# Attention by whole tiles beside the first product, with another order of decoding and another end

## The chip, the cores and the metric

One core of a Trainium2 chip runs the kernel. The metric is the device time of one execution in microseconds. TensorE multiplies matrices, VectorE and GpSimd compute element by element, ScalarE evaluates functions and copies, SyncE issues most transfers. Each engine works through its own instructions in order and waits on semaphores for the others.

## What is computed

Attention within chunks of 64 tokens, for 8 batches of 8 heads with 576 tokens of 64 values, and then two products with a function between them, twice:

```python
scores = scale * np.matmul(q_c, k_c.transpose(0, 1, 2, 4, 3))   # in chunks of 64
scores = scores - np.max(scores, axis=-1, keepdims=True)
attn = np.exp(scores)
attn = attn / (np.sum(attn, axis=-1, keepdims=True) + 1e-09)
out = np.matmul(attn, v_c)
# x: 4608 tokens x 512
h = x @ w_in; r = np.maximum(h, 0.0); x = (r * r) @ w_out       # 512 -> 2048 -> 512
h = x @ w_in2                                                    # 512 -> 2048
g = np.where(h >= 1, h, np.where(h <= -1, 0.0, (h + 1) ** 2 / 4))
return g @ w_out2                                                # 2048 -> 512
```

The weights arrive as float64 and are decoded from their bits in the kernel.

## The kernel before, in words

The tokens of the attention stand in 36 tiles of 128 tokens; a tile has two units of four heads each (`UT` = 2, 72 units). A unit goes through steps: A (`att_a`, line 285) transposes q and k with four 128x128 transposes into one PSUM bank; `att_ae` copies them out on ScalarE; B (`att_b`) makes the scores with sixteen 64x64 products and takes their maximum on VectorE; `att_exp` (line 322) makes four exponentials on ScalarE with their sums; `att_n` inverts the sums on VectorE and scales on GpSimd; C (`att_c`) transposes twice, `att_ce` copies out; D (`att_d`) weighs v with sixteen 64x64 products; `att_x` (line 374) splits the result on ScalarE and VectorE into a rounded part xh and a rest xl, the input of the first product.

The first product (`plain_h`, line 400) runs in 9 blocks of 512 tokens. For each of 16 pieces of weights (`fi`) it makes two slots of six products of 128x128 by 128x512, called ph in the profile; after the second slot ScalarE takes the relu into a buffer g, GpSimd squares it, and SyncE stores it. Two PSUM banks take turns (`h0`, `h1`); the g buffers are a ring of six (`RG`, line 397). The pieces of the first product's weights are decoded in three steps: `piece_a` (an absolute value on ScalarE and three bit operations on VectorE, lines 111 to 118), `piece_b` (a product on VectorE, line 147, and a cast on ScalarE, line 150), `piece_c` (a subtraction on GpSimd). One call of `decode` (line 671) takes step c of one piece, b of the next and a of the one after, and loads the piece two ahead into one of two staging buffers `ws`. The weights of the three later products are decoded in 48 units (m, a, b) in the same way (`unit_a` to `unit_d`, lines 174 to 219): four parts, three sums of them on GpSimd, a rounded part and a rest of seven columns, stored to DRAM and loaded by `load_w` (line 243) as tiles for TensorE when a product is near.

The order is written out by hand. A head of eleven turns does the attention of the first four tiles and the first decoding calls. Then a list of slots follows: slot 2 (16 j + fi) + c is one half of a product step of block j. In each slot come the six products, then a decoding call if one is due (`PACE`), then what `at_slot` has put there. A turn of one unit takes four slots: D, B and x in the first, the exponentials in the second, C with its copy and the normalization in the third, A with its copies and the loads of q, k and v in the fourth. Decoding units start at slot 22 (`U0`) and come every 5.1 slots.

```python
            if n_dec[0] < NF + 2 and n_dec[0] < len(DEC) + 1 + PACE * ((s + 2) // 2):
                decode()
```

The second product (`form_b`, w = 0), the third (`form_a`) and the fourth (`form_b`, w = 1) run after slot 288 (`SB1`) in five pairs of token halves with seven products each instead of eight (P1 to P7). At the end of the last, the result goes through `store` (line 600): VectorE transposes it in blocks of 32, and SyncE stores it in four transfers.

Of the kernel before, what the change touches and what calls it, by code (L numbers as in the profile page):

```python
# [15 lines left out]
P = 128  # L16

TINY = 2.0**-15 * 1.125
CH = 64
# [7 lines left out]
CIDX = {"P1": 0, "P2": 1, "P7": 2, "P4": 3, "P5": 4, "P6": 5, "P3": 6}  # L27
# [4 lines left out]
def chunk_attention_moe_moe2(ctx, tc, q, k, v, w_in1, w_out1, w_in2, w_out2, out):  # L32
# [72 lines left out]
    win = {}  # L105
    wst = {}
# [17 lines left out]
    def wy():  # L124
        n_y[0] += 1
        return rt(4 + n_y[0] % 3, [P, 4 * P], "wy", U32)
# [54 lines left out]
    def sums(c):  # L181

        for o, x, z, op in ((4, 2, 3, ALU.add), (2, 0, 2, ALU.subtract), (5, 4, 0, ALU.subtract), (6, 1, 5, ALU.subtract)):
            nc.gpsimd.tensor_tensor(out=c[:, o], in0=c[:, x], in1=c[:, z], op=op)
# [21 lines left out]
    def unit_c(*u):  # L206
        c = wst[u]
        hi = ep.tile([P, 7, P], F32R, tag="wh", name="wh", bufs=2)
        nc.scalar.copy(hi, c)
        wst[u] = (c, hi)  # L210

    def unit_hi(m, a, b):
        nc.sync.dma_start(out=wd[m, a][:, 0, b], in_=f(wst[m, a, b][1]))

    def unit_d(m, a, b):
        c, hi = wst.pop((m, a, b))
        lo = ep.tile([P, 7, P], F32R, tag="wl", name="wl", bufs=2)
        nc.vector.tensor_tensor(out=lo, in0=c, in1=f(hi), op=ALU.subtract)
        nc.sync.dma_start(out=wd[m, a][:, 1, b], in_=f(lo))
# [21 lines left out]
    wt = {}  # L241

# [7 lines left out]
    att = {}  # L250
# [45 lines left out]
    def att_ae(u):  # L296
        qkT = ep.tile([P, 2, NP, P], F32, tag="qkT", name="qkT", bufs=2)
        nc.scalar.activation(out=qkT[:, 0], in_=att[u][:, 0], func=AF.Copy, scale=SCALE)
        nc.scalar.copy(qkT[:, 1], att[u][:, 1])
        att[u] = qkT  # L300

    def att_b(u):

        qkT = att[u]
        pt = pa.tile([P, 2, 512], F32, tag="qk", name="psB")
        for p in range(NP):
# [9 lines left out]
        sc = pt[:, :, 0:2 * CH].rearrange("q e (c k) -> q e c k", c=2)  # L316
        m = ep.tile([P, 2, 2], F32, tag="m", name="m", bufs=3)
        z = ep.tile([P, 2, 2], F32, tag="z", name="z", bufs=3)
        nc.vector.tensor_reduce(out=m, in_=sc, op=ALU.max, axis=AX.X, negate=True)
        att[u] = [sc, m, z]  # L320

    def att_exp(u):
        sc, m, z = att[u]
        s = ep.tile([P, 2, 2, CH], F32, tag="s", name="s", bufs=2)
        for e in range(2):
            for c in range(2):
# [6 lines left out]
                )  # L333
        att[u] = [s, z]

    def att_n(u):
        s, z = att[u]
        nc.vector.tensor_scalar_add(z, z, 1e-9)
        nc.vector.reciprocal(z, z)
        s4 = s.rearrange("q e c k -> q (e c) k")  # L340
        z4 = z.rearrange("q e c -> q (e c)")
        nc.gpsimd.tensor_tensor(out=s4, in0=s4, in1=z4.unsqueeze(2).to_broadcast([P, HU, CH]), op=ALU.mult)

    def att_c(u):
        s, _ = att[u]
        pt = pa.tile([P, 2, NP, CH], F32, tag="t", name="psC", padded_shape=[P, HU, 2, CH], bufs=2)
        for e in range(2):
            nc.tensor.transpose(  # L348
                pt[:, e].rearrange("k p t -> k (p t)"), s[:, e].rearrange("q c k -> q (c k)"), ident
            )  # L350
        att[u] = pt

    def att_ce(u):
        at = ep.tile([P, 2, NP, CH], F32, tag="atT", name="atT", bufs=2)
        nc.scalar.copy(at, att[u])
        att[u] = at

    def att_d(u):

        at = att[u]  # L360
        pt = pa.tile([P, 2, 512], F32, tag="d", name="psD")
        for p in range(NP):
            for c in range(2):
                for e in range(2):
                    nc.tensor.matmul(  # L365
                        pt[rows(e), c, p * CH:(p + 1) * CH],
# [5 lines left out]
        att[u] = pt  # L372

    def att_x(u):
        pt = att.pop(u)
        (xh, xl), a, n = unit_x(u)[0]
        o = pt[:, :, 0:NP * CH].rearrange("d c (p t) -> d p c t", p=NP)
        xh, xl = (x.rearrange("d p (c t) -> d p c t", c=2) for x in (xh, xl))
        nc.scalar.copy(xh, o)
        nc.vector.tensor_tensor(out=xl, in0=o, in1=f(xh), op=ALU.subtract)  # L380
# [16 lines left out]
    RG = tuple(range(7, 13))  # L397
# [167 lines left out]
    def form_b(w, j, prod, kk):  # L565
# [20 lines left out]
        for dp in range(2):  # L586
            c = c_tile(n)
            if key is None:
# [11 lines left out]
    def store(j, dh, th, dp, c):  # L600
# [5 lines left out]
        for a in range(P // G):  # L606
            nc.sync.dma_start(
# [10 lines left out]
    LB, LC, LD, LV = 1, 2, 3, 0  # L618
    PER = 4
    DEC = (1, 2, 4, 6, 8, 10)  # L620
    PACE = 0.78
    U0, UPER = 22, 5.1
# [28 lines left out]
    with tc.manual_schedule():  # L651
# [14 lines left out]
        strokes = []  # L666
        for p in range(NF):
            strokes.append([(piece_a, p), (piece_b, p), (piece_c, p)])
        n_dec = [0]

        def decode():
            n = n_dec[0]
            n_dec[0] += 1
            if 0 <= n - 2 < NF:
                piece_c(n - 2)
            if 0 <= n - 1 < NF:
                piece_b(n - 1)
# [5 lines left out]
        def turn(i):  # L683

            res = [[] for _ in range(4)]

            def put(n, fn, u):
                if 0 <= u < NU:
                    res[n].append((fn, (u,)))

            put(0, att_d, i - LD)
            put(0, att_b, i - LB)
            put(0, att_x, i - LD)
            put(1, att_exp, i - LB)
            put(2, att_c, i - LC)
            put(2, att_ce, i - LC)
            put(2, att_n, i - LB)
            put(3, att_a, i)
            put(3, att_ae, i)
            if i >= LV and (i - LV) % UT == 0 and i - LV < NU:  # L700
                res[3].append((load_v, ((i - LV) // UT,)))
            if i % UT == UT - 1 and i // UT + QB < NU // UT:
# [197 lines left out]
```

## Time and profile before

| | |
|---|---|
| time, median of 3 runs | 1622.3 us (1620.76 to 1623.78) |
| time of the profiled execution | 1622.09 us |
| its span, first to last instruction | 1620.3 us |
| TensorE busy | 1586.6 us (98%) |
| VectorE, ScalarE, GpSimd busy | 1089.7, 868.5, 413.3 us |

Times in the rows below count from the start of the span. PE is TensorE, PEld its weight loads, DVE VectorE, ACT ScalarE, POOL GpSimd, SP SyncE. A busy TensorE is not one at its peak, since products are pipelined: starts matter more than durations. L451 is a line of the kernel.

### The profile page before, as it was taken

The numbers are of one execution on the slowest core, as the hardware profiler recorded it, in microseconds if no ns is written. First come the engines' busy times: TensorE is split into PE (matmuls) and PEld (weight loads), VectorE is DVE, ScalarE is ACT, GpSimd is POOL, SyncE is SP. The second block draws the span as 40 slices with busy tenths as digits, with TensorE's granted clock in tenths as the row PEclk, the third lists the DMA queues.
The fourth block names the chain that finished last, engine by engine and source line by source line (L and its number), as shares of the span: only waits on it lengthen the run. The fifth ranks groups of instructions, "written<-read, shape, count | busy, mean of one in ns | idle before, by whom it ended". The sixth has DMA issues, their size and how long they took to land.

```text
span 1620.3 us, 27342 instructions
## 1 busy us (share of the span) xinstructions
PE 1586.6 (98%) x9504; PEld 1362.6 (84%) x9504; DVE 1089.7 (67%) x1437; ACT 868.5 (54%) x1852; POOL 413.3 (26%) x461
## 2 busy tenths in 40 slices
PE   7889999999999999999999999999999999999998
PEld 5667777777778899999888898898888899998887
DVE  5956666665443376777677666857574787877786
ACT  7656666666553344344444566666665434444442
POOL 2657666665444200000000333333220000000000
PEclk9999999999999999999999999999999999999999
DMA  9769999999996982625378665574679773563723
GB/s 213 204 185 295 291 290 287 293 302 281 277 301 205 318 250 91 216 62 190 110 219 254 210 230 178 190 238 159 240 244 337 248 199 99 129 170 83 207 37 49
DMA packets 442730, 339.47 MB, mean 210 GB/s; under 512 B 214240, under 2 KB 419040, under 8 KB 442592
## 3 DMA queue, kind: packets, MB, share of 16 engines
q1 hardware_dynamic: 442592, 337.73, 69.3%
q8 instruction: 75, 1.23, 0.3%
q14 instruction: 63, 0.52, 0.1%
HBM read 195.04 MB, written 142.61 MB: 208 GB/s over the span
## 4 chain that ended last, share of the span: by engine, by line
PE 87%; DVE 5%; ACT 2%; DMA 2%; issue 2%; POOL 1%; SPq 0%; DVEq 0%; ACTq 0%; POOLq 0%
PE X L451 34%; PE ph L409 23%; PE V L451 17%; PE W L451 8%; PE psA L291 1%; PE psD L365 1%; PE psB L309 1%; DVE ol L441 1%; DVE t L532 1%; PE psC L348 1%; DMA ws<-in_moe_w_in_dram 1%; ACT s L327 1%; DVE wy L115 1%; DVE xr L445 0%; DVE wy L118 0%
## 5 line engine op out<-in xcount | busy, mean ns | idle before, releaser
L451 PE MATMUL X<-oh,w 128*128 128x448 f32 (+1 forms) x1920 | 557.5, 371 | 1.5 <-DVE c L512 1.5
L440 ACT CAST oh<-gr 128x896 fp32r<-128x896 f32 (+1 forms) x280 | 270.0, 964 | 334.1 <-PE X L451 160.5
L441 DVE TENSOR_TENSOR ol<-gr,oh 128x896 fp32r<-128x896 f32 (+1 forms) x280 | 314.5, 1124 | 182.6 <-ACT oh L440 175.3
L451 PEld LDWEIGHTS X<-oh,w 128*128 128x128 f32 x1920 | 360.0, 188 | 43.8 <-DVE c L512 1.9
L451 PE MATMUL X<-ol,w 128*128 128x448 f32 (+1 forms) x960 | 356.4, 371 | 4.2 <-DVE ol L441 4.2
L451 PE MATMUL V<-oh,w 128*128 128x448 f32 (+1 forms) x960 | 278.5, 371 | 0.0
L409 PE MATMUL ph<-xh,ih 128*128 128x512 f32 x576 | 245.3, 426 | 0.0
L409 PE MATMUL ph<-xl,ih 128*128 128x512 f32 x576 | 227.9, 396 | 0.0
L409 PE MATMUL ph<-xh,il 128*128 128x512 f32 x576 | 227.8, 395 | 0.0
L422 POOL TENSOR_TENSOR g<-g 128x512 f32<-128x512 f32 x144 | 171.3, 1189 | 143.6 <-ACT g L421 140.5
L451 PEld LDWEIGHTS X<-ol,w 128*128 128x128 f32 x960 | 180.1, 188 | 26.7 <-DVE ol L441 6.3
L451 PEld LDWEIGHTS V<-oh,w 128*128 128x128 f32 x960 | 180.2, 188 | 20.9
L445 DVE TENSOR_TENSOR gr<-gr,gr 128x896 f32<-128x896 f32 (+1 forms) x160 | 177.9, 1112 | 3.7 <-DMA gr<-g 3.7
L451 PE MATMUL V<-ol,w 128*128 128x448 f32 (+1 forms) x480 | 178.0, 371 | 0.0
L421 ACT ACTIVATE g<-ph 128x512 f32<-128x512 f32 x144 | 86.4, 600 | 134.8 <-PE ph L409 123.3
L451 PE MATMUL W<-oh,w 128*128 128x448 f32 (+1 forms) x480 | 139.4, 371 | 0.0
L409 PEld LDWEIGHTS ph<-xl,ih 128*128 128x128 f32 x576 | 109.3, 190 | 24.7
L409 PEld LDWEIGHTS ph<-xh,ih 128*128 128x128 f32 x576 | 109.4, 190 | 21.6
L409 PEld LDWEIGHTS ph<-xh,il 128*128 128x128 f32 x576 | 110.0, 191 | 16.6
L526 ACT ACTIVATE t<-c,half 128x448 f32<-128x448 f32 (+1 forms) x120 | 81.3, 681 | 70.9 <-DVE c L512 70.8
L441 POOL TENSOR_TENSOR ol<-xr,oh 128x896 fp32r<-128x896 f32 (+1 forms) x10 | 23.7, 2374 | 360.7 <-ACT oh L440 353.0
L532 DVE SCALAR_TENSOR_TENSOR t<-c,t 128x448 f32<-128x448 f32 (+1 forms) x120 | 96.4, 830 | 18.4 <-ACT t L526 18.2
(69 smaller groups left out, 1906.0 us busy)
## 6 DMA issues: line engine op xcount, KB each, us to landing
w<-w SPq DMA_DIRECT2D x168, 256.0 KB, 5.1
gr<-g SPq DMA_DIRECT2D x96, 448.0 KB, 5.2
gr<-g SPq DMA_DIRECT2D x64, 480.0 KB, 4.6
g<-t SPq DMA_DIRECT2D x96, 224.0 KB, 2.7
wu<-in_moe_w_out_dram SPq DMA_DIRECT2D x64, 256.0 KB, 4.6
g<-t SPq DMA_DIRECT2D x64, 240.0 KB, 4.4
w<-wh SPq DMA_DIRECT2D x32, 448.0 KB, 4.1
w<-wl SPq DMA_DIRECT2D x32, 448.0 KB, 5.0
```

The lines of the kernel that those rows point to most:

```text
L115: nc.vector.scalar_tensor_tensor(out=y, in0=w1, scalar=0xC0000000, in1=y, op0=ALU.bitwise_and, op1=ALU.bitwise_or)
L291: nc.tensor.transpose(pt[:, i, p, :], qkn[i][:, h0 + 2 * p:h0 + 2 * p + 2, :].rearrange("p h d -> p (h d)"), ident)
L309: nc.tensor.matmul(pt[rows(p), e, c * CH:(c + 1) * CH], qkT[rows(e), 0, p, rows(c)], qkT[rows(e), 1, p, rows(c)], start=True, stop=True,)
L409: nc.tensor.matmul(ph, win[fi][wi][:, kt * P:(kt + 1) * P], x[:, i, :], start=(kt == 0 and a == 0), stop=(kt == KT - 1 and a == 2),)
L421: nc.scalar.activation(out=g, in_=ph, func=AF.Relu)
L422: nc.gpsimd.tensor_tensor(out=g, in0=g, in1=g, op=ALU.mult)
L440: nc.scalar.copy(hi, raw)
L441: eng.tensor_tensor(out=lo, in0=raw, in1=f(hi), op=ALU.subtract)
L445: eng.tensor_tensor(out=o, in0=x, in1=z, op=ALU.subtract)
L451: nc.tensor.matmul(o, wt_[:, wi, c, :], x[:, i, :], start=first and a == 0, stop=last and a == 2, skip_group_check=True,)
L526: nc.scalar.activation(out=t, in_=h, func=AF.Square, bias=half, scale=0.5)
L532: nc.vector.scalar_tensor_tensor(out=t, in0=h, scalar=1.0, in1=t, op0=ALU.max, op1=ALU.min)
```

## The change

In the loop beside the first product attention goes by tiles of two units: eight transposes in A into two banks, 32 products in B and in D, four transposes in C, one maximum over both units, the exponentials in two groups of four, one normalization. A tile takes eight slots (`PER` = 8). D of a tile and B of the next stand in one slot, x and the first four exponentials in the same slot, the other four in the next, the normalization four slots after B, C six after, A four before the next B. The head does the first four tiles by units as before, and A, B and the exponentials of the fifth by a whole tile.

Decoding gets a step more: the cast on ScalarE (`piece_h`) and GpSimd's subtraction come one call later each. In a slot it now stands behind the attention. Seven calls fall in the head instead of six, `PACE` is 0.8 instead of 0.78, units start at slot 28 and come every 5 slots. A fourth buffer y comes from the ring of g, which keeps five. For the second product's weights (m = 0) the three products P1, P5 and P6 are written straight into TensorE's tiles by `unit_c` and `unit_d`; only the other four columns go to DRAM, and 24 of 168 loads fall away. In the last store of the kernel VectorE transposes from PSUM without a copy, and every second transfer is issued by ScalarE.

```diff
-CIDX = {"P1": 0, "P2": 1, "P7": 2, "P4": 3, "P5": 4, "P6": 5, "P3": 6}
+CIDX = {"P1": 0, "P2": 1, "P7": 2, "P4": 3, "P3": 4, "P5": 5, "P6": 6}
...
-        return rt(4 + n_y[0] % 3, [P, 4 * P], "wy", U32)
+        return rt(4 + n_y[0] % 4, [P, 4 * P], "wy", U32)
...
+    def piece_h(p):
+        y, hi, lo = wst[p]
         nc.scalar.copy(hi, f(y))
...
+    def unit_c(m, a, b):
+        c = wst[m, a, b]
+        if m == 0:
+            for prod in RANK[:3]:
+                if b == 0:
+                    wt[0, a, prod] = wp.tile([P, 2, 2, P], F32R, tag=f"w{w_tag(RANK.index(prod) * HF + a)}", name="w0")
+                nc.scalar.copy(wt[0, a, prod][:, 0, b], c[:, CIDX[prod]])
+        r = unit_r(m)
+        hi = ep.tile([P, r.stop - r.start, P], F32R, tag="wh", name="wh", bufs=2, padded_shape=[P, 7, P])
+        nc.scalar.copy(hi, c[:, r])
+        wst[m, a, b] = (c, hi)
+    def unit_r(m):
+        return slice(1, 5) if m == 0 else slice(0, 7)
...
+        if m == 0:
+            for prod in RANK[:3]:
+                t = wt[0, a, prod]
+                nc.vector.tensor_tensor(out=t[:, 1, b], in0=c[:, CIDX[prod]], in1=f(t[:, 0, b]), op=ALU.subtract)
+        lo = ep.tile([P, r.stop - r.start, P], F32R, tag="wl", name="wl", bufs=2, padded_shape=[P, 7, P])
+        nc.vector.tensor_tensor(out=lo, in0=c[:, r], in1=f(hi), op=ALU.subtract)
+        nc.sync.dma_start(out=wd[m, a][:, 1, b, r], in_=f(lo))
...
+    def tile_a(t):
+        att[t, "a"] = []
+        for i in range(2):
+            pt = pa.tile([P, UT, NP, P], F32, tag="t", name="psA", bufs=2)
+            for h in range(0, H, 2):
+                nc.tensor.transpose(
+                    pt[:, h // HU, h // 2 % NP, :], qks[t][i][:, h:h + 2, :].rearrange("p h d -> p (h d)"), ident
+                )
+            att[t, "a"].append(pt)
...
+    def tile_b(t):
+        pt = pa.tile([P, 2, 512], F32, tag="qk", name="psB")
+        for i in range(UT):
+            scores(pt[:, :, i * 2 * CH:(i + 1) * 2 * CH], qkT_of(t * UT)[:, i])
+        att[t, "b"] = maxima(pt, UT * 2)
+    def tile_exp(t, e):
+        exps(s_of(t * UT), *att[t, "b"], (e,), UT * 2)
...
-    RG = tuple(range(7, 13))
+    RG = tuple(range(8, 13))
...
+            if key is None and w == 1 and j == NPAIR - 1:
+                store(j, dh, th, dp, o[dp])
+                continue
...
-            nc.sync.dma_start(
+            (nc.scalar if j == NPAIR - 1 and th == 0 and a % 2 else nc.sync).dma_start(
...
-    PER = 4
-    DEC = (1, 2, 4, 6, 8, 10)
-    PACE = 0.78
-    U0, UPER = 22, 5.1
+    PER, PH = 8, 4
+    DEC = (1, 2, 3, 5, 7, 9, 10)
+    PACE = 0.8
+    U0, UPER = 28, 5
...
+            for d, fn in ((3, piece_c), (2, piece_h), (1, piece_b)):
+                if 0 <= n - d < NF:
+                    fn(n - d)
...
+        for t in range(T0_, NTI):
+            g = PER * (t - T0_ - 1) + PH
+            if t > T0_:
+                at_slot(g - 4, tile_a, t)
+                at_slot(g - 4, tile_ae, t)
+                at_slot(g - 4, load_v, t)
+                if t + QB < NTI:
+                    at_slot(g - 4, load_qk, t + QB)
+                at_slot(g, tile_b, t)
+                at_slot(g, tile_x, t - 1)
+                at_slot(g, tile_exp, t, 0)
+                at_slot(g + 1, tile_exp, t, 1)
+                at_slot(g + 4, tile_n, t)
+            at_slot(g + 6, tile_c, t)
+            at_slot(g + 6, tile_ce, t)
+            at_slot(g + PER, tile_d, t)
+        at_slot(g + PER, tile_x, t)
...
-            s = 2 * NF * (NBL - 3) + 2 * t if t < 24 else 2 * NF * (NBL - 1) + 2 * (t - 24) + 1 if t < 32 else SB1 + t - 30
-            at_slot(s, load_w, 0, tag, kk, RANK[r])
+            if t >= 24:
+                s = 2 * NF * (NBL - 1) + 2 * (t - 24) + 1 if t < 32 else SB1 + t - 30
+                at_slot(s, load_w, 0, tag, kk, RANK[r])
...
-            if n_dec[0] < NF + 2 and n_dec[0] < len(DEC) + 1 + PACE * ((s + 2) // 2):
-                decode()
             i = 0
...
+            if n_dec[0] < NF + 3 and n_dec[0] < len(DEC) + 1 + PACE * ((s + 2) // 2):
+                decode()
```

## Rows read from the trace of the kernel before

**Rows 1.** Windows: stretch, TensorE and other engines' busy us, granted clock, DMA share, GB/s.
```profile
39.00:130.00 91.00, 79.88 (x661) 62.13 (x658) 68.60 (x106) 53.75 (x175) 56.95 (x55) 0.92 0.69 198
130.00:500.00 370.00, 370.00 (x3232) 293.37 (x3223) 222.17 (x406) 232.26 (x797) 218.53 (x274) 1.00 0.95 289
551.50:1613.10 1061.60, 1055.92 (x5040) 944.51 (x5039) 764.11 (x858) 538.20 (x729) 106.61 (x96) 1.00 0.60 181
```

**Rows 2.** TensorE's timeline (start, us, what, idle before), chain (start, us), a window.
```profile
52.71 0.70 PE L365 MATMUL psD<-atT,vt 64*64 64x64 f32 x16 [3.67 <-ACT atT L355]
...
98.97 0.73 PE L309 MATMUL psB<-qkT 64*64 64x64 f32 x16 [5.01 <-ACT qkT L299]
...
54.47 5.06 PE ph L409 x12
...
99.70 4.67 PE ph L409 x12
...
54.40:59.00 4.60, 4.60 (x15) 3.63 (x12) 4.53 (x6) 2.36 (x10) 3.74 (x3) 0.50 0.53 163
```

**Rows 3.** VectorE's groups, 39 to 100 (busy us, mean ns), and ScalarE's timeline.
```profile
L118 DVE SCALAR_TENSOR_TENSOR wy<-ws,wy 128x512 uint32<-128x512 uint32 x11 | 12.0, 1087 | 0.4
L115 DVE SCALAR_TENSOR_TENSOR wy<-ws,wy 128x512 uint32<-128x512 uint32 x11 | 11.7, 1065 | 0.4
L112 DVE TENSOR_SCALAR wy<-ws 128x512 uint32<-128x512 uint32 x11 | 10.5, 957 | 1.0 <-DMA ws<-in_moe_w_in_dram 1.0
L147 DVE SCALAR_TENSOR_TENSOR wy<-ih,wy 128x512 f32<-128x512 f32 x11 | 8.7, 794 | 0.1
...
97.22 0.67 ACT L111 ACTIVATE wa<-wu 128x512 f32<-128x512 f32 x1 [4.49 <-DMA wu<-in_moe_w_out_dram]
```

**Rows 4.** Chain of waits near the loop's end (start us, us, what).
```profile
487.10 1.39 PE ph L409 x6
488.49 0.44 PE psA L291 x4
488.93 1.40 PE ph L409 x6
490.32 0.39 PE psD L365 x16
490.71 0.29 PE psB L309 x14
491.00 2.95 PE ph L409 x12
493.95 0.22 PE psC L348 x2
494.17 2.77 PE ph L409 x12
496.94 0.39 PE psD L365 x16
```

**Rows 5.** Head: chain (start, us) and TensorE's timeline.
```profile
13.86 1.29 ACT s L327 x8
...
29.42 0.73 PE L309 MATMUL psB<-qkT 64*64 64x64 f32 x16
...
39.01 0.79 PE L409 MATMUL ph<-xh,ih 128*128 128x512 f32 x1
```

**Rows 6.** End: chain (start, us) and SyncE's queue.
```profile
1613.12 0.57 ACT c L589
...
1613.77 4.09 SPq L607 DMA_DIRECT2D out_dram<-ct  x8
```

**Rows 7.** Groups from 130 to 500 (busy us, mean ns, idle before).
```profile
L421 ACT ACTIVATE g<-ph 128x512 f32<-128x512 f32 x105 | 63.0, 600 | 89.3 <-PE ph L409 84.5 <-DMA g<-g 3.0 <-DMA qkn<-in_k_dram 1.5
...
L342 POOL TENSOR_TENSOR s<-s,z 128x256 f32<-128x256 f32 x52 | 42.8, 823 | 32.0 <-DVE z L339 13.3 <-PE ph L409 6.1 <-PE psA L291 3.8
...
L319 DVE TENSOR_REDUCE m<-psB 128x4 f32<-128x256 f32 x52 | 22.0, 422 | 76.2 <-PE psB L309 76.0
```

More of the change, by code (lines that the diff above doesn't have):

```diff
@@ L105, in chunk_attention_moe_moe2, with w_tag @@
     win = {}
+    wt = {}
+    def w_tag(t):
+        return (t + 2 * NF) % 56
     wst = {}
@@ L246, in load_w, with of_tile, qkT_of, s_of @@
         wt[m, a, prod] = t
-    att = {}
+    att, ttile = {}, {}
+    def of_tile(name, u, shape, bufs=1):
+        if (name, u // UT) not in ttile:
+            ttile[name, u // UT] = ep.tile(shape, F32, tag=name, name=name, bufs=bufs)
+        return ttile[name, u // UT]
+    def qkT_of(u):
+        return of_tile("qkT", u, [P, UT, 2, NP, P])
+    def s_of(u):
+        return of_tile("s", u, [P, 2, UT * 2, CH], SBUFS)
+    def at_of(u):
+        return of_tile("atT", u, [P, UT, 2, NP, CH])
     def rows(par):
@@ L315, in att_b, with maxima, exps @@
                     )
[L316 to L318 removed]
+    def maxima(pt, n):
+        sc = pt[:, :, 0:n * CH].rearrange("q e (c k) -> q e c k", c=n)
+        m = ep.tile([P, 2, n], F32, tag="m", name="m", bufs=3, padded_shape=[P, 2, UT * 2])
+        z = ep.tile([P, 2, n], F32, tag="z", name="z", bufs=3, padded_shape=[P, 2, UT * 2])
         nc.vector.tensor_reduce(out=m, in_=sc, op=ALU.max, axis=AX.X, negate=True)
[L320 to L326, printed above, removed]
+        return [sc, m, z]
+    def exps(s, sc, m, z, es, n):
+        for e in es:
+            for c in range(n):
                 nc.scalar.activation(
@@ L351, in att_c, with tile_c, tile_ce @@
         att[u] = pt
     def att_ce(u):
-        at = ep.tile([P, 2, NP, CH], F32, tag="atT", name="atT", bufs=2)
-        nc.scalar.copy(at, att[u])
-        att[u] = at
+        nc.scalar.copy(at_of(u)[:, u % UT], att[u])
+    def tile_c(t):
+        att[t, "c"] = pt = pa.tile([P, UT, 2, NP, CH], F32, tag="t", name="psC", bufs=2)
+        for i in range(UT):
+            turned(pt[:, i], s_of(t * UT), i)
+    def tile_ce(t):
+        nc.scalar.copy(at_of(t * UT), att.pop((t, "c")))
     def att_d(u):
-        at = att[u]
@@ L681, in decode @@
                     stage_piece(n + 2)
[L683 to L702, printed above, removed]
-                res[3].append((load_qk, (i // UT + QB,)))
-            return res
         def tiles_until(j):
@@ L720, in head @@
             do(att_d, i - LD)
+            if i == n0:
+                tile_a(T0_)
             do(att_exp, i - LB)
             do(att_ae, i)
+            if i == n0:
+                tile_ae(T0_)
             do(att_ce, i - LC)
+            if i == n0 + 1:
+                for e in range(2):
+                    tile_exp(T0_, e)
             if i in DEC:
```

120 lines of the change are left out of this document (66 added, 54 removed).

## The prediction

> **What bounds the kernel now.** I read busy time by stretch first, then the waits of TensorE, then the chain of waits where TensorE stands still. From 551.5 to 1613.1 TensorE is busy 1055.9 of 1061.6 us [rows 1]: the second and third products leave under 6 us, and the change hardly touches their order. From 130 to 500 it is busy 370.0 of 370.0 us [rows 1]. So there only fewer or shorter TensorE instructions help. From 39 to 130 it is busy 79.9 of 91.0 us [rows 1]: 11.1 us of waits in the first block. In that block the reader is to see two long waits, 3.67 us for a copy of atT and 5.01 us for qkT, both late on ScalarE [rows 2]. Behind each the granted clock falls to 0.50, the 1.2 GHz level: twelve products then take 5.06 and 4.67 us [rows 2], against 2.95 at full clock [rows 4]. That is 2.1 + 1.7 = 3.8 us more, so the first block loses 14.9 us in all. ScalarE is late because its in-order queue holds a decoding step that waits for VectorE, and VectorE spends 0.957 + 1.065 + 1.087 + 0.794 = 3.9 us on each of eleven pieces between 39 and 100 [rows 3]. For the second wait it holds the first step of a unit, which stood 4.49 us for its load [rows 3].
>
> **Whole tiles.** One unit's turn on TensorE is read from one stretch of the chain. D takes 0.39 us, B behind it 0.29, and the twelve products after them 2.95 where twelve after a C take 2.77: 0.18 more [rows 4]. Where D runs alone it is 0.39 again, so the sixteen small products of B are worth 0.29, and D, which has sixteen of the same size, about 0.29 + 0.10. Entering and leaving the 64x64 form therefore costs 0.10 + 0.18 = 0.28 us a time. C (two transposes) takes 0.22. A (four) takes 0.44 and the products around it 1.39 + 1.40 instead of 2.77 [rows 4], about 0.46: both are near 0.11 a transpose, with next to nothing per group. So a tile of two units saves one 0.28 and nothing on transposes: 31 tiles x 0.28 = 8.7 us. One D that stood alone goes too (0.28). Against it, the loop gets one more A and one more C, since the head did eleven A and nine C and will do ten and eight: 0.46 + 0.22 = 0.7. Net **-8.3 us**. Ends: nothing saved, +0.7, if a block of 64 small products costs as much as two of 32; and -13, if the transposes share 0.07 a group as well. I take the middle value, since B's 0.29 was read with and without a neighbour.
>
> **New waits in that loop.** At full clock a slot of six products is 2.77 / 2 = 1.39 us. The exponentials of half a tile now stand on ScalarE ahead of the relu of the pair of slots that ends next, where one unit's four stood behind it; behind them wait that relu, its square on GpSimd, and the PSUM bank that TensorE wants again three slots (4.2 us) after B. The maximum over twice the width takes up to 2 x 0.42 us [rows 7], four exponentials 1.29 [rows 5], a relu 0.60 [rows 7]: 2.7 us. So VectorE may come 1.4 us late before TensorE stands. It sat idle before 52 maxima for 76.2 us in all, 1.5 each [rows 7], so it is mostly early. The other wait: the normalization is issued at the tile's slot + 4 and C at + 6, 2.8 us apart. GpSimd needs 2 x 0.82 = 1.6 us for it [rows 7], and a square or the four sums of a unit may stand ahead. With sums right before it C waits about 1 us; the period of five slots against eight puts them there in one unit of eight, four times. I take **+1.0 us** for this stretch, ends 0 and +31 (1 us at each tile).
>
> **First block.** Units now start at slot 28 instead of 22, behind the last decoding, and their first loads two to three slots ahead of that. So the 4.49 us wait for the load on ScalarE goes, with the late GpSimd and SyncE work around it. Attention stands ahead of decoding in a slot, and ScalarE's cast of a piece comes one call later than VectorE's product for it, so ScalarE no longer stands for a product just issued. What is late next is VectorE itself. Seven decoding calls fall in the head and one each in slots 0, 1, 2, 4, 6. From 41 us on VectorE has four first parts (3 x about 1.04 = 3.1 us each) and three second parts (0.8) ahead of the maximum of slot 4 [rows 3], 14.8 us, and 1.2 of attention: it comes at 57. TensorE ends that B at 41 + 1.3 (half clock at the start) + 5 x 1.39 + A 0.92 + C 0.44 + 1.44 = 52. Late by 5 us, less the 1.4 of slack: a wait of about 3.5 us. At slot 12 VectorE has 13.9 us more and TensorE 3.5 + 8 x 1.39 + 2.8 = 17.4: on time. A wait of 3.67 us brought the lower clock [rows 2], so I add half of its 2.1 us: 4.5 us are left of 14.9, **-10.4 us**. Ends: all goes, -14.9, and none, 0. The ring of g buffers falls from six to five, 17 instead of 21 us for relu, square and store; in the first block a store came late in SyncE's queue, which counts for the upper end. Decoding loads of ws stay two ahead and stand in the same queue as the g stores, as now.
>
> **Head.** In the head a decoding call more (eight to ten: seven calls for six) and a tile's A and B replace three units' A and two units' B. From the B at 29.42 to the first product at 39.01 it is 9.6 us now [rows 5]. After the change: B 0.73, maximum 0.42, exponentials 1.29 and about 0.4 of decoding; the copies of eight transposes (four take 0.44 at full clock [rows 4], twice that here) end about 4.2 us after that B; then a B of twice 0.73, a maximum of 0.84, eight exponentials 2.6, two decoding steps on ScalarE 1.2, xh and xl 0.8, D 0.7: 11.8 with overlaps taken off about 11.5. **+1.9 us**, ends 0 and +4.
>
> **In-place weights.** For 24 tiles of the first three products the loads (256 KB each) fall away, and the stores of 16 units shrink from seven columns to four. ScalarE gets three copies of a 128x128 for each unit and a cast over four instead of seven, VectorE three subtractions. No load of a weight ends a TensorE wait between 130 and 551, and ScalarE and VectorE are busy 232 and 222 of 370 us there [rows 1], so the added work, at most 0.7 us for 16 units, is covered: 0. Uncovered it would be +10; if a transfer gets clear of it, -1.
>
> **End.** The last two copies to SBUF go (0.57 on the path [rows 6]), as VectorE transposes from PSUM, and every second of the eight last stores is issued by ScalarE. Now SyncE issues eight in 4.09 us, 0.51 each [rows 6], and the span ends 2.4 us after the last issue. Halved, 2.0 us go if issuing sets the pace, none if the transfers do. Between 0.6 and 2.6 I take **-2.0**, nearest to the issue row. The Trainium skill's page DMA: Bandwidth & Descriptors (Issuing engines are not separate DMA queues) says the contrary in weight: all issuers share the same sixteen DMA engines, and a second issuer saves only the sequencer's time, usually small. Here issue was 4.09 us of the last 7.2, so the trace agrees only in the mechanism; by the page's "small" the sum would be 1605.5.
>
> **The sum.** The profiled run took 1622.1 us by the clock of the times (span 1620.3), 0.2 under the median 1622.3. 1622.1 - 8.3 - 10.4 + 1.0 + 1.9 + 0 - 2.0 = 1604.3: forecast **1604**.
>
> **Rivals.**
> 1. VectorE stays the bound of the first block. For: 3.9 us a piece, and five calls nearly in a row at the loop's start. Against: units no longer overlap with decoding. Nothing is gained there: 1604 + 10.4 = 1614.
> 2. The first block runs without a wait and transposes share their group cost: 1604 - 4.5 - 4.5 = 1595. For: attention is ahead of decoding in each slot. Against: the maximum is still queued behind earlier slots' decoding.
> 3. Slower: relu behind exponentials. In each tile VectorE comes late with the maximum, the exponentials hold the relu, and TensorE stands for the bank. The gains without the loop's new waits are 19 us, so it decides from 19 / 31 = 0.6 us a tile. At 1.5 us a tile: 1604 - 1 + 46 = 1649; at 0.8, 1628. Against: no wait of TensorE in 370 us now, and 1.5 us of idle time ahead of a maximum.
> 4. The change doesn't do what it says: a merged B and D still drain at every unit. Then 8.7 + 0.3 us stay: 1613.
>
> **Chances.** Forecast 0.53 (its own range 1598 to 1610), rival 1 0.15, rival 2 0.14, rival 4 0.08, rival 3 0.10. The range 1593 to 1618 takes in all but rival 3 and the edges of the others. A difference of 0.2%, 3.2 us, is about what can be told here. Faster 0.86 (all but rival 3, less 0.04 of stray in rivals 1 and 4), same 0.05, slower 0.09.
>
> **What would show it.** Right: D and B in one block of 64 small products near 1.4 us, and a period of a tile near 13.8 us where two turns take 14.1; TensorE waits under 6 us between the first product and 130, and none of 5 us; first product of weights near 41; last transposes right behind the last product and the span ending about 5 us later. Wrong: waits of the first kind of product for a relu in every tile, waits of C for the normalization, or a granted clock of 0.50 behind a wait after 60 us.

## The result, and the profile after

The changed kernel takes 1635.1 us (median of 4 runs, 1630.9 to 1636.7), the kernel before beside it 1622.0 (1620.8 to 1623.8): 1.0079 of the time before, 95% interval 1.0065 to 1.0092. It is slower by 13 us where the forecast was 18 us faster. The profiled execution has a span of 1633.4 us against 1620.3.

First the windows that answer to [rows 1] (columns as there):

```profile
39.00:130.00 91.00, 77.52 (x668) 61.62 (x669) 64.79 (x91) 53.25 (x177) 50.27 (x45) 0.98 0.67 182
130.00:500.00 370.00, 352.94 (x3117) 285.08 (x3115) 233.64 (x364) 228.25 (x742) 219.26 (x248) 0.99 0.88 251
564.10:1627.10 1063.00, 1056.49 (x5041) 944.59 (x5039) 765.18 (x858) 537.70 (x728) 106.87 (x96) 1.00 0.60 181
```

The reader is to see the middle row: TensorE, busy for all of these 370 us before, now stands 17 us of them. The third row, 1063.0 against 1061.6 us, is nearly as it was. The names in the rows: psA to psD are the PSUM tiles that steps A to D write, qkT and atT ScalarE's copies of A and C; s are the exponentials, z the sums and their inverse; wu is a unit of weights as loaded, wa its absolute value, wc its four parts and three sums. What TensorE waits for stands in its waits (waiting line, what it waits for: us in total, times, longest):

```profile
PE psC L420 <- POOL s L395: 21.8, 19, 2.4
PE ph L506 <- ACT g L518: 5.6, 2, 4.6
...
PE psD L451 <- DVE xl L467: 3.9, 2, 3.4
...
PE psD L451 <- ACT atT L438: 1.9, 1, 1.9
```

The wait of the transposes C for GpSimd's normalization is new in this size: before it was 1.4 us in four.

```profile
PE psC L348 <- POOL s L342: 1.4, 4, 0.4
```

TensorE's timeline gives the rest of the account, by the start of B in three tiles (start us, us, what; the windows end inside B, so durations and counts are not those of its 32 products):

```profile
54.26 0.45 PE L366 MATMUL psB<-qkT 64*64 64x64 f32 x15
...
75.00 0.56 PE L366 MATMUL psB<-qkT 64*64 64x64 f32 x20
...
407.47 0.73 PE L366 MATMUL psB<-qkT 64*64 64x64 f32 x31
```

And the chain of waits where nothing disturbs it, which answers to [rows 4] (start us, us, what):

```profile
455.90 2.74 PE ph L506 x12
458.64 0.44 PE psC L420 x4
459.08 2.77 PE ph L506 x12
461.85 0.62 PE psD L451 x32
462.48 0.57 PE psB L366 x29
463.05 5.69 PE ph L506 x24
468.74 0.87 PE psA L345 x8
469.61 2.74 PE ph L506 x12
```

A tile's period is 469.61 - 455.90 = 13.71 us. D and B are one block of 1.19 us, where two units took 2 x (0.39 + 0.29) = 1.36 [rows 4]. From 75.00 to 407.47 there are 22 tiles; at 13.71 they would take 301.6 us and they take 332.5, so **30.8 us** are lost. The first tile, 54.26 to 75.00, takes 20.74: **7.0 us** lost. Of the 30.8, TensorE stands 22.4 us; the lower clock behind two of the waits takes some 3.6 more, and the rest is not resolved. The account of the 13.1 us, profiled run against profiled run:

| stretch | forecast | measured |
|---|---|---|
| head: first product at 43.60, before 39.01 | +1.9 | +4.6 |
| whole tiles: loop (520.5, before 512.3) less its losses (37.8, before 14.9) | -8.3 | -14.7 |
| first block's losses (7.0, before 14.9) | -10.4 | -7.9 |
| waits and lost clock from 75 to 407 us | +1.0 | +30.8 |
| second to fourth products (1063.0, before 1061.8) | 0 | +1.3 |
| last matmul to the end (6.3, before 7.2) | -2.0 | -0.9 |

The loop ends with the first instruction of the second product, at 564.08 us after and 551.33 before. The rows split at 75 us, where the forecast's first block ran to 130: some 6 of the 30.8 us lie between 75 and 130. On the forecast's own stretch the first block still loses about 13 of its 14.9 us, and the loop behind it about 25. One row is wrong by far. Its mechanism is read in one tile: timelines of VectorE, ScalarE, GpSimd and TensorE from 151 to 165 us (start us, us, what, idle time before and what ended it):

```profile
152.30 0.69 DVE L378 TENSOR_REDUCE m<-psB 128x8 f32<-128x512 f32 x1 [2.49 <-PE psB L366]
152.91 0.41 DVE L467 TENSOR_TENSOR xl<-psD,xh 128x256 fp32r<-128x256 f32 x1
...
158.30 0.69 DVE L205 SCALAR_TENSOR_TENSOR wc<-wa,wy 128x512 f32<-128x512 f32 x1 [1.12 <-ACT wa L117]
158.91 1.01 DVE L393 TENSOR_SCALAR z<-z 128x8 f32<-128x8 f32 x1
```

```profile
151.74 0.37 ACT L466 CAST xh<-psD 128x256 fp32r<-128x256 f32 x1 [1.44 <-PE psD L451]
153.35 0.38 ACT L466 CAST xh<-psD 128x256 fp32r<-128x256 f32 x1 [1.24 <-DVE xl L467]
...
157.55 0.71 ACT L117 ACTIVATE wa<-wu 128x512 f32<-128x512 f32 x1
```

```profile
159.85 2.80 POOL L193 TENSOR_TENSOR wc<-wc 128x128 f32<-128x128 f32 x4
162.62 1.08 POOL L395 TENSOR_TENSOR s<-s,z 128x512 f32<-128x512 f32 x1
```

```profile
163.76 0.65 PE L420 MATMUL psC<-ident,s 128*128 128x128 f32 x4 [1.91 <-POOL s L395]
```

Two things are late. First GpSimd: the four sums of a unit (2.80 us) stand in its queue ahead of the normalization. Then the chain that leads there: ScalarE's rounding of the second unit's values waits 1.24 us for VectorE's subtraction of the first, which itself stands behind the maximum; the exponentials, and a unit's first step behind them at 157.55, come later by that; VectorE waits 1.12 us for this step and has 1/z queued behind it. Together they use up the 2.8 us between normalization and C and cost TensorE 1.91; experiments 1 to 3 take them away one at a time.

### The profile page after: what moved, and what is told of

Read it like the earlier page. It is cut to its first block, busy times and chain, and to the rows that moved or that the text cites. A ratio compares the mean times of both kernels' runs of the same rounds, so it can differ in the third digit from the quotient of the medians.

```text
span 1633.4 us, 26997 instructions
## 1 busy us (share of the span) xinstructions
PE 1577.5 (97%) x9504; PEld 1361.9 (83%) x9504; DVE 1105.4 (68%) x1389; ACT 867.7 (53%) x1802; POOL 411.2 (25%) x429
## 4 chain that ended last, share of the span: by engine, by line
PE 79%; DVE 6%; DMA 3%; issue 3%; ACT 3%; POOL 3%; SPq 1%; POOLq 0%; DVEq 0%; ACTq 0%
PE X L548 34%; PE V L548 17%; PE ph L506 15%; PE W L548 8%; ACT s L384 1%; PE psC L420 1%; POOL s L395 1%; PE psD L451 1%; POOL g L519 1%; PE psB L366 1%; DVE t L629 1%; DVE ol L538 1%; DMA wu<-in_moe_w_in_dram 1%; POOL wc L193 1%; PE psA L345 1%
## 5 line engine op out<-in xcount | busy, mean ns | idle before, releaser
L506 PE MATMUL ph<-xh,ih 128*128 128x512 f32 x576 | 237.4, 412 | 5.7 <-ACT g L518 5.6
L519 POOL TENSOR_TENSOR g<-g 128x512 f32<-128x512 f32 x144 | 167.8, 1166 | 193.5 <-ACT g L518 163.8
L548 PEld LDWEIGHTS X<-ol,w 128*128 128x128 f32 x960 | 180.1, 188 | 26.9 <-DVE ol L538 6.7
L629 DVE SCALAR_TENSOR_TENSOR t<-c,t 128x448 f32<-128x448 f32 (+1 forms) x120 | 96.5, 831 | 18.6 <-ACT t L623 18.1
```

Of the source, the lines that this page charges most:

```text
L506: nc.tensor.matmul(ph, win[fi][wi][:, kt * P:(kt + 1) * P], x[:, i, :], start=(kt == 0 and a == 0), stop=(kt == KT - 1 and a == 2),)
L519: nc.gpsimd.tensor_tensor(out=g, in0=g, in1=g, op=ALU.mult)
L548: nc.tensor.matmul(o, wt_[:, wi, c, :], x[:, i, :], start=first and a == 0, stop=last and a == 2, skip_group_check=True,)
L629: nc.vector.scalar_tensor_tensor(out=t, in0=h, scalar=1.0, in1=t, op0=ALU.max, op1=ALU.min)
```

## The experiments

Times are medians, to be held against 1635.1 (after) and 1622.0 (before); the ratios are against runs of the kernel before on the same chip.

**1. The sums behind the normalization.** Units whose second step falls just ahead of it:

```diff
+        elif unit_slot(m, a, b) % PER in (PH, PH + 1):
+            late_sums[m, a, b] = c
         else:
             sums(c)
...
+                at_slot(g + 4 - p, unit_s, *u)
```

> The kernel after, but for the weights' units whose second step falls just ahead of a tile's normalization (two of the five places in a tile's turn): their four sums on GpSimd are issued at the slot of the normalization, behind it, and no work is left out. Theory A (the transposes of the probabilities wait because the sums, 2.8 us, stand ahead of the normalization in GpSimd's queue): the waits of psC for POOL's s of 1.7 to 2.4 us in two of five tiles shrink below 0.8, the loop from 75 to 407 us loses 15 to 25 us of its 31 us of waits and lost clock, time 1610 to 1620. Rival B (normalization is late because VectorE's 1/z stands behind ScalarE's relu and copies): the sums' place hardly matters, waits stay above 1.4 us, time 1631 to 1636. Rival C (the wait is only handed on: the unit's copies now wait on ScalarE for the sums, and the copy of psC stands behind them): psC's waits go but psD waits for ScalarE's atT by about as much, time 1625 to 1636.

Measured 1623.1 us, 1.0003 (0.9992 to 1.0015). Of 30.8 us, 18.1 are left from 75 us to the tile at 409. B said the place hardly matters: it falls as the whole cause. C's handing on is seen in size 0.2 to 0.5 us (psD for atT), and TensorE now waits for a relu 1.4 to 1.8 us in every fifth tile. But 18 us left, and the time, are more than A expected.

**2. The same, with those units' copies moved back too** (against experiment 1).

```diff
                 if p < 2:
                     at_slot(g + 4 - p, unit_s, *u)
-                    d = 0
+                    d = 2 - p
...
                 at_slot(g + 4 + d, unit_c, *u)
```

> As the kernel with late sums, and in those units the copies on ScalarE, the two stores and the subtraction on VectorE are moved two slots back too, behind the transposes' copy out of psC. No work is left out. Theory A: 1608 to 1618 us, psC waits under 0.8 us and psD waits none. Rival B (VectorE late behind ScalarE): the unit's three or four copies of 0.3 us no longer stand ahead of ScalarE's copy, but the max and 1/z are where they were: 1629 to 1636. Rival C (handed on to ScalarE in the kernel with late sums alone): this kernel is 5 us or more below that one.

Measured 1617.5 us, 0.9966 (0.9951 to 0.9981); 12.9 us left. It is 5.6 us below experiment 1, as C said: the units' copies, waiting for the later sums, had held ScalarE's queue.

**3. Rounding both units before both subtractions.**

```diff
         for i in range(UT):
-            x_parts(pt, t * UT + i, i * NP * CH)
...
+            nc.scalar.copy(xh, src)
+            parts.append((xl, src, xh))
+        for xl, src, xh in parts:
+            nc.vector.tensor_tensor(out=xl, in0=src, in1=f(xh), op=ALU.subtract)
```

> The kernel after, but the two units of a tile's weighted values are rounded by ScalarE one behind the other, and VectorE's two subtractions follow, where after has copy, subtraction, copy, subtraction. In the trace of after ScalarE's second copy waits 1.3 us for VectorE's first subtraction in 32 tiles (42.9 us in all). No work is left out. Theory A (GpSimd's sums make the normalization late): exponentials start 1.3 us earlier but the sums stand where they did, so of the 31 us of waits at most 5 go: 1629 to 1636 us. Rival B (ScalarE's chain of copy, exponentials, relu, copies makes 1/z late): the whole chain moves up 1.3 us, the waits of 1.7 to 2.4 us in two of five tiles shrink by 1 us or more, over some 24 waits and the clock's falls behind them: 1610 to 1622.

Measured 1624.2 us, 1.0008 (0.9994 to 1.0021); 19.6 us left. A expected at most 5 us from this and falls as the whole cause, and B's 1610 to 1622 is missed by 2: ScalarE's 1.3 us in each tile is worth 11 of the 31. Both subtractions and both roundings read the same tile psD; the traces show the wait between them, not its reason.

**4. Both.**

> The kernel with late sums and late copies of those units, and the order copy, copy, subtraction, subtraction of the two units' values besides. No work is left out. Theory (two causes with a share each: GpSimd's queue and ScalarE's chain ahead of 1/z): the tiles from 75 to 407 us lose 11 to 12 us with the late sums alone and about 20 with the order alone; with both 3 to 7, time 1609 to 1614. Rival (the two shorten the same wait, so the second adds nothing): 1616 to 1619.

Measured 1608.2 us (1608.1 to 1608.5), 0.9912 (0.9898 to 0.9927): 26.9 us below after, faster than before, and just under the theory's 1609 to 1614. The single gains, 17.6 and 10.9, nearly add up. TensorE's busy time from 75 to 407 us, first after, then with both:

```profile
75.00:407.00 332.00, 309.58 (x2713) 248.16 (x2704) 211.96 (x330) 206.13 (x670) 208.71 (x245) 0.99 0.86 244
```

```profile
75.00:407.00 332.00, 329.06 (x2944) 268.57 (x2939) 229.31 (x356) 221.97 (x723) 220.25 (x253) 1.00 0.93 265
```

and the waits of TensorE that are left with both:

```profile
PE psC L431 <- POOL s L406: 4.7, 8, 1.4
...
PE psD L462 <- DVE xl L478: 3.9, 2, 3.4
PE ph L525 <- ACT g L537: 3.8, 2, 3.6
```

Lost time and device time move together: 30.8, 18.1, 12.9, 19.6, 4.8 us lost for 1635.1, 1623.1, 1617.5, 1624.2, 1608.2. So 26 of the 30.8 us are these two orders (with the copies of experiment 2). Of the 4.8 that are left, one wait of 1.4 us at 86 us comes ahead of the units, so no sums stand there: it is for VectorE's late 1/z.

**5. The other parts, undone one at a time.** The weights made in place (`unit_r` gives all seven columns, the loads of t < 24 come back):

> The kernel after without the parts of weights made in place: all 7 parts of every unit are copied in one instruction, stored and loaded back, at the slots of the kernel before; the rest as after. No work is left out. Theory (the waits are those of sums and ScalarE's order): one long copy takes the place of three or four short ones, the waits of psC stay above 1.5 us in two of five tiles, time 1632 to 1637. Rival D (the short copies and subtractions of the first 16 units, on ScalarE and VectorE, make the chain of each tile late between 130 and 250 us): the waits fall by 0.5 us or more there and not behind 270 us, time 1626 to 1631.

Measured 1633.7 us, 1.0067 (1.0050 to 1.0084), not told apart from after; psC still waits 1.8 us and the loop is 520.1 us. D falls. The end:

```diff
-            (nc.scalar if j == NPAIR - 1 and th == 0 and a % 2 else nc.sync).dma_start(
+            nc.sync.dma_start(
```

> The kernel after with the end of the kernel before: the last pair's P4 is copied out of PSUM by ScalarE ahead of VectorE's transposes, and SyncE's queue alone issues all stores. No work is left out. Theory: the new end is worth the 0.9 us by which the stretch from the last matmul to the end of the span became shorter, so 1635.5 to 1637, and this stretch is 7.0 to 7.4 us again. Rival (the stores' bytes set the pace and the second queue does nothing): within 0.3 us of after, 6.2 to 6.6 us from the last matmul to the end.

Measured 1638.4 us, 1.0097 (1.0082 to 1.0112), and 7.5 us from the last matmul to the end of the span against 6.3: the new end is worth 0.9 to 1.2 us in the profiles, which the times (3.3 us apart, run to run about as much) don't make finer. The edit takes back the second queue and the copy of 0.57 us together, so it doesn't show what either is worth. And the decoding order (a slot's step goes ahead of its attention again besides):

```diff
-            for d, fn in ((3, piece_c), (2, piece_h), (1, piece_b)):
+            if 0 <= n - 1 < NF:
+                piece_b(n - 1)
+                piece_h(n - 1)
```

> The kernel after with the decoding of the kernel before: VectorE's product and ScalarE's rounding of a piece in one step and not two, and a slot's decoding step issued ahead of the slot's attention, not behind it. No work is left out. Theory (the new order brings a little in the first block, and nothing from 100 us on): the first tile's 20.7 us grow to 21 to 25, the rest as after, time 1635.5 to 1640. Rival (decoding behind the attention is what makes relu and the maxima late): first tile 16 to 19, time 1630 to 1634.

Measured 1639.0 us, 1.0118 (1.0101 to 1.0135). The first tile takes 16.0 us, which is the rival's number, but its B stands behind a wait of 4.09 us for atT and the next tile, with 3.68 for the normalization, takes 21.3; the first product starts 1.2 us later and the third B at 97.6 against 91.0. Time and loop go the theory's way: the new decoding order, its two parts together, helps by some 4 us, and the rival falls.

**6. The head and the first block.** In the head eight exponentials stand ahead of the rounding of unit 6 on ScalarE; moved behind it:

```diff
-            if i == n0 + 1:
+            if i == n0 + 2:
+                att_x(n0 - 1)
                 for e in range(2):
                     tile_exp(T0_, e)
-            if i in DEC:
+                decode()
+            if i in DEC and i != n0 + 1:
                 decode()
...
```

> The kernel after, but in the last turns ahead of the first product the eight exponentials of the first whole tile and one decoding step are issued behind the rounding of unit 6's weighted values, not ahead of it. No work is left out. Theory (the 3.39 us wait of unit 7's psD for VectorE's xl, behind these exponentials, is 2.7 of the 4.6 us by which the first product starts late): the first product starts at 40 to 41 us in place of 43.6, time 1631 to 1634. Rival (the exponentials come later, and so the first block's maxima, normalization and its one 4.6 us wait for relu grow by as much): the first product starts early, the second product starts where it did, time 1634.5 to 1637.

Measured 1637.9 us, 1.0087 (1.0070 to 1.0104). The first product starts at 40.23, as the theory said, but the second starts at 566.6, 2.5 us later than after's: the rival holds, and a little more. TensorE's waits of this kernel in the first block:

```profile
39.60 0.70 PE L451 MATMUL psD<-atT,vt 64*64 64x64 f32 x16 [0.95 <-DVE xl L467]
...
49.18 0.66 PE L420 MATMUL psC<-ident,s 128*128 128x128 f32 x4 [2.26 <-POOL s L395]
...
65.58 0.79 PE L506 MATMUL ph<-xh,ih 128*128 128x512 f32 x1 [4.44 <-ACT g L518]
```

A decoding step put off past the tile's maximum:

```diff
-            if n_dec[0] < NF + 3 and ...
+            if s not in (2, 3) and n_dec[0] < NF + 3 and ...
```

> The kernel after, but no decoding step is issued in slots 2 and 3 of the first block; the step that stood there comes behind the whole tile's maxima, and the steps behind it in the slots that follow. No work is left out. In the trace of after the tile's max starts at 59.85 us, 4.9 us behind the end of its scores, as VectorE is in decoding steps until then, and relu and the product wait 4.58 us. Theory (the place of one decoding step ahead of the max costs the first block's wait and the clock behind it): the wait falls below 1.5 us, the tile of 20.74 us to 14.5 to 17, time 1629 to 1632. Rival (VectorE is the first block's bound, the step that is put off is missed later): a wait of the product for the block's weights of 3 us or more appears between 60 and 90 us, time 1634 to 1638.

Measured 1637.0 us, 1.0090 (1.0075 to 1.0105). The wait of 4.58 us becomes three, and B starts again at 75.7:

```profile
59.70 0.50 PE L506 MATMUL ph<-xh,ih 128*128 128x512 f32 x1 [1.31 <-ACT g L518]
65.52 0.50 PE L506 MATMUL ph<-xh,ih 128*128 128x512 f32 x1 [1.91 <-ACT g L518]
70.42 1.11 PE L420 MATMUL psC<-ident,s 128*128 128x128 f32 x4 [2.86 <-POOL s L395]
```

The time is the rival's, but the wait that came back is for the normalization, not for weights. One decoding step more in the head, in VectorE's idle 4.84 us (`DEC = (1, 2, 3, 5, 7, 8, 9, 10)`, with the other head):

> The kernel with the head in the other order (the whole tile's exponentials behind the rounding of unit 6's values), and one more decoding step in turn 8, ahead of the whole tile's copies, so that eight stand ahead of the first product and not seven. No work is left out. In the trace of after VectorE is idle for 4.84 us in that turn (32.9 to 37.8) and then busy with decoding to 75 us. Theory (VectorE's steps of decoding bound the first block, so what the head wins comes back as waits for them unless its idle time is used): the first product starts at 40 to 41.5 us as in the kernel with the head alone, and the second product 2 to 5 us earlier than after's 564.1, time 1629.5 to 1633. Rival (the first block is bound by the chain max, exponentials, relu, wherever the decoding stands): second product at 564 to 567, time 1634.5 to 1638.

Measured 1638.3 us, 1.0108 (1.0095 to 1.0122), second product at 567.3: the theory fails, and the rival's numbers nearly come. On top of both orders, without and with the step put off:

> The kernel with late sums and copies and the order copy, copy, subtraction, subtraction (1608.2 us), with the head and the further decoding step of the kernel above. No work is left out. Theory: the head's 2 to 5 us come off it as well, 1603 to 1606.5. Rival (they don't add up, as the first block's wait is the same one): 1607 to 1610.

> The kernel above, and no decoding step in slots 2 and 3 of the first block. No work is left out. Theory (VectorE's total of decoding bounds the first block, and the place of one step only moves the wait, as it did from relu to the normalization in after): within 1.5 us of the kernel above. Rival (with one more step done ahead of the first product there is now room to put one off): 2 to 4 us below it.

Measured 1609.9 us, 0.9931 (0.9917 to 0.9944), and 1612.2, 0.9939 (0.9927 to 0.9952): neither is below the 1608.2 of both orders alone. Five tries to start earlier or to move a decoding step only moved the wait.

**7. What holds the first block.** On both orders mended, the low part is subtracted by VectorE:

```diff
-        nc.gpsimd.tensor_tensor(out=lo, in0=f(y), in1=f(hi), op=ALU.subtract)
+        nc.vector.tensor_tensor(out=lo, in0=f(y), in1=f(hi), op=ALU.subtract)
```

> The kernel with both orders mended (late sums and copies; copy, copy, subtraction, subtraction: 1608.2 us), and the low part of each decoded piece is subtracted by VectorE and not by GpSimd. No work is left out. Theory E (VectorE is the first block's bound because its steps take 1.4 to 1.7 us beside GpSimd in place of 0.42 to 0.69): a step grows by one subtraction of 0.4 to 0.7 us and loses 1 to 2 us of stretching, the first tile's 20.2 us fall to 16 to 18.5, time 1603.5 to 1606.5. Rival F (the staged piece's load is the bound): the wait of relu behind ScalarE's step for ws stays, first tile 19.5 us or more, time 1607 to 1610.

Measured 1606.5 us (1605.6 to 1608.8), 0.9903 (0.9886 to 0.9919). The first tile takes 17.5 us in place of 20.2, as E said, but starts 1.0 us later, so its end comes 1.6 us earlier (73.2 against 74.9); the time, 1.7 us lower, is within the intervals. VectorE's groups from 43.6 to 100 us (busy us, mean ns | idle before), first after, then this kernel:

```profile
L121 DVE SCALAR_TENSOR_TENSOR wy<-ws,wy 128x512 uint32<-128x512 uint32 x10 | 11.7, 1172 | 0.3
L118 DVE TENSOR_SCALAR wy<-ws 128x512 uint32<-128x512 uint32 x10 | 10.3, 1025 | 0.0
L153 DVE SCALAR_TENSOR_TENSOR wy<-ih,wy 128x512 f32<-128x512 f32 x10 | 9.9, 992 | 0.4
L124 DVE SCALAR_TENSOR_TENSOR wy<-ws,wy 128x512 uint32<-128x512 uint32 x10 | 9.6, 960 | 0.3
```

```profile
L163 DVE TENSOR_TENSOR il<-wy,ih 128x512 fp32r<-128x512 f32 x13 | 11.4, 874 | 0.0
L153 DVE SCALAR_TENSOR_TENSOR wy<-ih,wy 128x512 f32<-128x512 f32 x11 | 10.0, 913 | 0.0
L121 DVE SCALAR_TENSOR_TENSOR wy<-ws,wy 128x512 uint32<-128x512 uint32 x10 | 8.4, 836 | 0.3
L124 DVE SCALAR_TENSOR_TENSOR wy<-ws,wy 128x512 uint32<-128x512 uint32 x10 | 7.6, 765 | 0.3
L118 DVE TENSOR_SCALAR wy<-ws 128x512 uint32<-128x512 uint32 x10 | 5.8, 585 | 0.0
```

With 12 of GpSimd's instructions gone VectorE's are shorter: five steps a piece take 4.0 us by their means (874 + 913 + 836 + 765 + 585 ns), where four took 4.1 (and 4.1 with both orders alone: 1179 + 997 + 912 + 1057). Three buffers for the staged pieces, without that:

```diff
-        t = ep.tile([P, 4 * P, 2], U32, tag="ws", name="ws", bufs=2)
+        t = ep.tile([P, 4 * P, 2], U32, tag="ws", name="ws", bufs=3)
```

> The kernel with both orders mended (1608.2 us), and three buffers in place of two for the staged pieces and units, so that a load no longer waits for the piece just being decoded. No work is left out. Rival F (loads of ws bind): ScalarE's waits for ws of 1.1 to 2.8 us between 44 and 60 us fall below 0.5, first tile 16 to 18.5 us, time 1603.5 to 1606.5. Theory E (VectorE binds): VectorE is as busy as before (30 of 32 us from 43 to 75), first tile within 1 us of 20.2, time 1607 to 1609.5.

Measured 1607.9 us, 0.9910 (0.9895 to 0.9925), first tile 20.2 us as without, though ScalarE's wait for ws there fell from 2.48 to 0.95 us: F falls. Last, the other head on VectorE's subtraction, and all of it:

> The kernel with both orders mended and VectorE's subtraction, with the head's other order besides (the exponentials of the first whole tile and one decoding step behind the rounding of unit 6's values), by which the first product started 3.4 us earlier. No work is left out. Theory E: with VectorE relieved the head's 3.4 us come through by 1.5 to 3: that much below the kernel without the head's order. Rival F: they come back as a wait, within 1 us of that kernel.

> All of the above together: both orders mended, VectorE's subtraction, three buffers for the staged pieces, the head's other order. No work is left out. Theory E: the third buffer adds nothing, within 1 us of the kernel without it. Rival F: it is 2 us or more below that kernel. Either way the fastest of the four if both have a share: 1599 to 1604.

Measured 1608.6 us, 0.9914 (0.9899 to 0.9928), and 1609.9 (1605.9 to 1612.1), 0.9919 (0.9899 to 0.9938). Neither is below the 1606.5 without the head's order: the head's gain comes back even here, by more than F's 1 us, and the 1599 to 1604 expected of all together are missed; there the first tile takes 20.6 us, with one wait of 4.43 for relu. So E holds for the first tile without the third buffer (17.5 and 18.6 us), and an earlier first product helps no kernel: in all of them the second B comes at 73 to 80 us. The traces show a reason that the experiments don't separate. VectorE is busy 27.0 to 28.4 of the 29 us from 44 to 73 in each of these kernels, and the head's order also moves a decoding step back, so the steps that stand ahead of the first tile's maximum in VectorE's queue start later. The first of them, in after and then with the head's order alone:

```profile
39.33 0.42 DVE L118 TENSOR_SCALAR wy<-ws 128x512 uint32<-128x512 uint32 x1
```

```profile
41.72 0.42 DVE L118 TENSOR_SCALAR wy<-ws 128x512 uint32<-128x512 uint32 x1
```

The maximum then comes at 61.36 in place of 59.85. A head that starts the product earlier and these steps no later was not tried.

## Why the prediction was wrong, step by step

**New waits in the loop: the step that failed.** The forecast took +1.0 us, from "C waits about 1 us" in "one unit of eight, four times", and gave +31 as the upper end. Measured are 30.8. Both factors were wrong. The count: the sums stand ahead of the normalization in two places of eight, not one; of the 32 units with sums eight meet a tile there, not four. The price: seven of these eight tiles wait 1.8 to 2.4 us for the normalization, and the eight lose 22 us in all, 2.8 each, because the forecast let the normalization start at its slot, 2.8 us ahead of C, while 1/z came later than that: ScalarE's two roundings, with a wait between them, and the unit's steps in its queue were counted nowhere. The other tiles lose the remaining 8 to 9 us. Behind two of these waits the clock falls: after 2.39 us the granted clock is 0.58 for 4 us, and the tile loses 4.2 (as after one of 1.88; after the others it stays at 1.00).

```profile
193.98:198.00 4.02, 4.02 (x13) 3.35 (x14) 2.23 (x3) 0.94 (x2) 0.99 (x1) 0.58 1.01 218
```

Experiments 1 to 4 show both causes, 17.6 and 10.9 us. The eighth tile lost its time another way: ScalarE stood 5.01 us for a unit's load, which the forecast of the first block had called gone, and D waited 1.89 behind it.

```profile
119.49 0.67 ACT L117 ACTIVATE wa<-wu 128x512 f32<-128x512 f32 x1 [5.01 <-DMA wu<-in_moe_w_out_dram]
```

With both orders the load still costs ScalarE 2.83 us and TensorE next to nothing.

**Whole tiles.** Right in kind, too small: 0.43 us a tile (2 x 7.07 = 14.14 before, 7.07 being 494.17 - 487.10 in [rows 4]; 13.71 after) against the 0.28 taken. The block of D and B is shorter than four pieces by 0.17, and one entry less into the twelve products is worth 0.2. 0.43 x 31 is 13.3 of the 14.7; the rest is not resolved. Rival 4, in which units still drain one by one, falls.

**First block.** -7.9 to 75 us, and about -2 to 130 us, against -10.4. The wait forecast at slot 8, about 3.5 us as VectorE is late, is there with 4.58 us. VectorE's lateness was right: the maximum starts at 59.85 and TensorE ends B at 54.94, 4.9 us apart as forecast, both 3 us later than worked out, mostly because the head ended 2.6 us later than the 41 taken. The slack behind it was not: from the maximum's start to the relu's end it takes 4.2 us in place of 2.7, as ScalarE's second rounding and two decoding steps stand between. The clock behind the wait (0.56 from 64.1 to 68) cost about 2 us where 1 was added. Then came the waits from 75 to 130, 5.4 us, that the forecast had none of: with them TensorE waits 10.1 us between the first product and 130, where under 6 was the sign of being right. Rival 1 (VectorE stays the bound, nothing gained) is nearer than the forecast.

**Head.** +4.6 against +1.9. The sum put ScalarE's 2.6 us of exponentials beside the rest; in the queue they stand ahead of unit 6's rounding, and D of unit 7 waits 3.39 us. Mending it won 3.4 us there and nothing at the end, so the experiments don't show that this row's excess cost anything by itself.

**In-place weights**: 0, as forecast (experiment 5). **End**: -0.9 against -2.0. SyncE's and ScalarE's queues after, and then how long one of the last eight stores takes to land, before and after (count, KB, median us):

```profile
1627.20 2.38 SPq L708 DMA_DIRECT2D out_dram<-ct  x4
...
1627.21 2.46 ACTq L708 DMA_DIRECT2D out_dram<-ct  x4
```

```profile
out_dram<-ct SPq DMA_DIRECT2D x8, 60.0 KB, 1.9
```

```profile
out_dram<-ct SPq DMA_DIRECT2D x4, 60.0 KB, 3.0
out_dram<-ct ACTq DMA_DIRECT2D x4, 60.0 KB, 3.2
```

Issuing fell from 4.09 [rows 6] to 2.4 us, 1.6 to 1.7 of the 2.0 forecast, and the copy of 0.57 is gone besides; but a store now takes 3.0 to 3.2 us to land in place of 1.9, and the span ends 3.7 us after the last issue in place of 2.4. That gives back 1.3 of the 2.2. The eight transfers are spread over about 4.4 us before and 3.9 after (an estimate from the DMA slices of the last 7 us), so they bound the end nearly as much as issuing did. The "small" saving that the prediction cites from the Trainium skill was nearer than the full one; the 1605.5 that it puts beside it, for which it shows no working, is as far off.

**Rival 3**, the slower one, had the right sign by another place. Relu did not bind: TensorE waited for it twice, 5.6 us. The price at which it decides, 0.6 us a tile, was passed (1.4 us a tile, 30.8 / 22) by a wait it doesn't name.

## What to carry to other kernels

Where two periods beat against each other (units every five slots, tiles every eight), list every coincidence of a beat and what stands in each in-order queue ahead of the step on the path; then give a slack once, to one engine, not to each. A wait with an upper end of 31 us and a value of 1 wants its count worked out before anything else. And a pair of engines that hand work to and fro (copy, subtract, copy, subtract) may be cheaper as copy, copy, subtract, subtract: here 10.9 us of 1635 for an exchange of two lines.

## What the runs showed of the hardware

The same VectorE instruction (L118, 128x512 uint32) takes 0.42 us alone, up to 1.5 beside GpSimd's subtractions and 1.27 beside its scaling and squaring; its mean between 43.6 and 100 us, 1025 ns after and 997 with both orders, was 585 when the twelve subtractions went. The Trainium skill, Perfetto Trace Analysis (Optimizing Scalar/DVE Operations), says that GpSimd and VectorE share a read port, so that moving work between them might not help. The traces agree in that VectorE's instructions are longer beside GpSimd's; the port itself they don't show. Here moving work to the busier of the two shortened the first tile by 2.6 us, and the kernel by no more than the intervals allow.
